# A new written-out order of steps, new evacuation engines and a new table of array parts for a fused H3 and FFN kernel on one core

## The chip, the core and the metric

The kernel runs on one core of a Trainium2 chip. A core has five engines that take instructions in order, each from its own queue: PE (TensorE, matmuls into PSUM), ACT (ScalarE, activation functions and copies), DVE (VectorE, elementwise work), POOL (GpSimd, some elementwise work and the issue of some DMAs) and SP (SyncE, here the issue of most DMAs). They wait for each other through semaphores. The metric is the device time of one execution in microseconds, lower is better.

## The reference

Inputs are `q`, `k`, `v` of 2048 x 640 in bfloat16, small filters, and the weights of a feed-forward net with 1728 hidden units. `_B_setup`'s own input is not used: both parts take the normalised `q`.

```python
xn = _layernorm(A_q)
# part A: H3
k_shift = sum over t of k_pad[t:t+S] * shift_k[ks-1-t]     # 4 taps
kv = k_shift * v
y = irfft(rfft(kv, 2S) * rfft(ssm_k, 2S))[:S] + kv * ssm_D  # long causal convolution
s = xn * y
# part B: FFN
g = silu(gelu(xn @ w1 + b1) @ w2 + b2)
return A_q + s * g
```

## The kernel before

**The opening.** `prologue` loads the first quarter of `q` and `w1`, normalises that quarter, transposes it and runs the first six column blocks of the first FFN matmul. On POOL it also computes, in `small_second`, the phases `ph` and the masks from which the 32 x 32 matrices of the short transform (`mats`) are made. The change leaves the opening as it is.

**The steps.** Everything behind the opening is one long string, `PLAN`, of 1190 steps. A loop at the end of the kernel calls one small function for each step, in the order written. Each engine's queue, and with it the order in which each engine works, is thus the order of the plan; so is which PSUM bank (of eight, `ones`) and which SBUF slot (`slots`) a step gets, since they are taken from and given back to lists as the steps are called. A step's name is a kind, a number and, where two engines can do it, the engine: `a` is ACT, `d` is DVE. `evac` (L145 to L148) does such a copy out of PSUM on the one or the other.

The kinds that matter here, with the lines of the profile of before:

- Layer norm of chunks 1 to 3 (a chunk is a quarter of the rows): `ls` statistics (DVE, L418 and L419), `lv`, `lr` (POOL), `lb`, `ln` the normalising itself (ACT L439 or DVE L441), `tt` transposes (PE L448), `te` their copy out (L147 or L148).
- FFN: `h` one column block of the first matmul (PE, L464; the last and narrow one of a chunk L460), `he` its gelu (ACT, L476 and L473), `g` one half row block of the second matmul (PE, L497, 14 matmuls), `ge` its silu (ACT, L505), `gm` the product with xn (DVE, L512). `h` and `g` steps 0 to 13 and 0 to 7 are those of chunk 0, and so on.
- Convolution filter: `kt` transposes of `ssm_k` (PE, L536), `kc` their copy out, `kf` the long first transform (PE, L547), `ke` its copy out, `ks` store to the DRAM scratch `scrK` (POOL), `fl` load back (SP), `ff` the short transform in 32-row blocks (PE, L411), `fe` its copy out, `mk` a copy with neighbouring rows swapped (SP).
- `kv`: `cv` the 64 steps of taps and products (DVE, L580, L587, L591), `em` and `ee` the taps spread over the partitions, then `uf`, `ue`, `us` (scratch `scrU`), `ml`, `mu` as for the filter.
- Spectrum and inverse: `mp` and `mq` the two products (DVE, L671), `ma` and `mb` the short inverse in 32-row blocks (PE, L411), `me` its copy out, `ms` store to `scrC` (POOL, L701), `yl` load back (SP, L708), `y` the long inverse (PE, L716 and L717), `yt` the product with xn * g (DVE, L725), `yo` and `ga` the last additions, `ys` and `gs` the stores.
- Tables of sines: `w` the phase of the first transform (`f1_phase`, DVE, L308), `ws` its sines (ACT), `s` the phase of `mats` (`small_phase`, DVE, L381 and L382), `ss` its sine (ACT, L387), `sm` the multiplication with the masks (DVE, L391). `ip`, `ia` (DVE, L618, L622) and `is`, `ib`, `ic` (ACT, L626, L630, L634) make the four tables of the last inverse, where `ia` needs `ip`.

**What binds the order.** All 16 `ks` stores must be in `scrK` before any `fl` load, and likewise for `scrU` and `scrC`, because the scratch is written by rows of one kind and read by rows of another. So no `y` can begin before the last `me` has been stored and read back. Gelu and silu lie in different tables of ACT; each change from one to the other is an `ACT_TABLE_LOAD`.

**The array parts.** A step of 32-row blocks is four matmuls of 32 x 32, one for each strip of rows, each on one of the 16 parts of the array. `TURNS` gives for each of the 48 column tiles which parts these are:

```python
for i in range(P // QB):
    j = (i + int(TURNS[turn])) % (P // QB)
    a, b = (slice(x * QB, (x + 1) * QB) for x in ((i, j) if m == F2 else (j, i)))
    nc.tensor.matmul(out=out[b, :], lhsT=mats[a, m, a], rhs=rhs[a, :], start=start, stop=stop)
```

Of the kernel before, what the change touches and what calls it, by code (L numbers as in the profile page):

```python
# [36 lines left out]
lv1 s cv8 cv17 cv9 he6 lr1 lb1 C4 he13 ee6.a cv18 cv19 cv10 ln4.d h10 he11 he10 h7 he7 h12 h9 ln5.a he12 ln7.a ln6.d  # L37
cv0 cv20 tt9 tt7 C1 C3 C0 he9 C2 cv11 cv1 te7.d cv21 ws0 tt6 tt8 te8.d g1 tt5 te9.d ss sm cv12 cv2 cv3 te5.d K3 X2 V5
K2 V4 V0 V3 V6 g0 ws1 ws2 ge0 ge1 g2 ge2 d kt1 kt7 kt6 kc7.a kt3 kt0 cv22 cv4 te6.d kc6.d kt2 kt9 kc3.d kc2.d kc0.a V2
X3 V7 kc9.d kc1.a kt12 kt4 kf2 kf23 kt11 kf8 ke2.d kc12.a V1 kt13 kc4.d kc13.d kf0 ke23.a ke8.a gm0.d kf6 kf22 ke6.a  # L40
ke22.a kt5 kf10 kf38 kc11.d ke0.d kt8 kf4 kc8.d kc5.d ke10.a ke38.a kf9 kt10 ke9.a ke4.a kt15 kc15.d kc10.d kt14 kf1
kf17 kc14.a kf11 kf40 ke17.a ke40.a kf15 kf29 kf18 kf21 ke11.a ke18.a ke15.a cv32 gm2.d cv13 gm1.d ke29.a g3 ke21.a
ke1.a kf45 kf7 kf5 kf35 kf20 ke45.a ke5.a kf19 ke19.a ke7.a ke35.a ke20.a ge3 kf16 g4 kf3 ge4 ke3.a ks7 ks0 ks2 kf39
kf37 cv24 ks6 ks1 ke39.a ke37.a kf27 cv33 cv23 cv34 cv5 cv35 ls10 gm3.d cv25 cv36 cv48 kf14 kf25 ke16.a ke27.a ke25.a
# [12 lines left out]
ff25 ue23.a fe12.a ff16 ff28 ff13 ff8 ff6 ff21 fe13.a fe6.a ff23 ff43 fe8.a fe28.a ff35 fe25.d fe2.d fe16.d us7 ff7
fe23.d fe21.d ff46 ff15 ff31 fe43.a fe7.a ln8.d gm10.d ls14 fe15.a fe46.a fe35.a fe31.a us12 gm9.d ln11.d g11 ge11 ff9
ff3 ff47 ff10 fe10.a fe47.d fe3.d ff4 ff33 ff20 fe33.a fe20.a tt13 ff24 fe24.a fe4.a mk2 fe9.d te13.d ff11 tt11 tt14
fe11.a te14.d tt10 te11.d te10.d ml2 ls13 ff34 ff29 ff1 ff37 fe34.a fe37.a ml1 ml3 mk1 ff44 ff14 ff42 fe14.d mk3 ml4  # L60
ml0 fe42.a fe29.a tt12 fe1.a te12.a fe44.a ls15 g12 gm11.d lv3 lr3 ge12 ml8 mu7 mp7 ff0 mu6 ff26 ff27 ff32 mu8 mp6
fe0.a fe32.a fe27.a fe26.a mp8 mq8 mq7 mq6 g14 mu11 ff45 ff17 ff18 mu9 fe45.a lb3 fe17.a fe18.a ln14.a g13 mp9 mp11
mq11 mq9 ge13 mu5 ge14 ma8 mb8 mu4 ma7 ff19 mb7 ff30 mu10 mp5 mp4 mq5 gm12.d mk8 mk4 mq4 g15 me8.a fe19.a fe30.a
ln15.a me7.a mk0 mu12 ff36 mu13 ma9 mu25 mp10 mb9 mu24 ge15 mq10 mp12 mq12 mp24 mq24 mp13 mq13 mp25 h39 h29 fe36.a
he39 me9.a he29 h28 ma11 mu26 mu14 ma5 mu2 mb5 mq25 mb11 ln13.a h30 ml5 ml6 ml7 mk6 fl13 he28 me5.a h32 he30 me11.a
ma24 mu3 ma10 mu18 mb24 mb10 mk5 mk7 ml9 mk12 q5 mk9 mp14 mp2 mp26 mq26 mq2 he32 me24.a ln12.a h40 mk14 ml11 he40
me10.a mp3 mp18 mq14 mq18 mq3 h34 ma2 mu19 mu23 mp23 ff41 mb2 he34 mq23 ff40 mu16 ff39 fe41.a fe40.a me2.a fe39.a h31
mu15 mu1 ma18 ma13 mb13 mb18 mp19 mq19 h41 mp1 mp16 mq1 he31 me18.a he41 me13.a mp15 h35 he35 ma4 mq16 mu17 ma12 ml12
mb4 mp17 mb12 me4.a me12.a h36 ma14 ma19 mu0 mq17 mb19 mq15 ma6 ma16 mu22 mb16 mb14 mb6 he36 mp0 mq0 me19.a me16.a
me6.a me14.a h37 mu27 ma15 ma26 mb26 mb15 mu28 mu21 h33 mp22 mq22 me26.a he37 he33 mp27 mp28 mq28 ml13 me15.a mq27  # L70
mk10 h38 he38 mp21 mq21 tt15 mu20 ma1 mb1 ml14 mu40 mp20 mp40 mu38 mk13 ml15 q2 q6 me1.a tt16 tt19 tt17 g17 te17.a
te16.a te19.a te15.a mp38 ma38 mq38 mb38 ma40 ma28 gm13.d mq40 mq20 mu43 mu37 me38.a ma3 mb28 mb40 mb3 mu41 g16 me40.a
me28.a me3.a mp37 mq37 mp43 mk11 ma27 ml10 mu35 mp41 mq41 ge16 gm14.d ma0 ma17 mb27 mb0 mb17 mu34 me0.a me17.a gm15.d
mp35 mp34 mq34 ge17 me27.a mk15 q0 g18 mq43 ge18 mq35 gm17.d ma25 ma23 mu36 ma34 mb25 mb23 mb34 mp36 mu29 mu31 tt18
me34.a me25.a me23.a te18.a mp29 gm16.d mq29 mq36 mp31 mq31 g19 ma21 mu32 q3 ma29 ma41 mu47 mb21 mb29 mb41 g20 me29.a
mp47 mq47 me41.a ge19 ma20 mu39 ma37 ma36 me21.a mu30 mb37 mb20 mb36 mp32 mq32 ir ge20 g21 ma32 mp39 me37.a me20.a
me36.a ma39 mu33 ma43 mp30 mq39 gm18.d mq30 ge21 mb32 ma31 ma47 mb39 ms0 ms5 ms3 ms9 ms2 ms8 ms1 ms12 mb43 mb31 mb47
mu45 g22 me39.a me31.a me47.a ms4 me43.a me32.a ms6 ms13 ma35 gm19.d mp33 mq33 mp45 mq45 ma33 ma22 ip1 ia1 ma30 mb35
mb33 mb22 ge22 mb30 mu42 mu44 mu46 me22.a me35.a me33.a me30.a ms7 is1 ib1 h43 h53 h50 mp42 mp46 mp44 mq42 mq44 mq46
ma44 ms10 ma42 ma45 gm21.d ma46 mb44 mb42 mb45 mb46 ms11 me46.a me44.a ic1 me45.d me42.d g23 gm20.d h48 h42 he42 h46  # L80
he50 h49 h55 he49 he48 h44 he46 h52 he43 he52 h51 he44 he51 he55 h54 ms14 gm22.d h45 ms15 yl5 he53 he54 he45 h47 yl7
yl6 y11 y9 y10 ip2 he47 g24 yl12 yl4 q1 yl1 yl2 ip3 ip0 ia2 yt11 ia0 ia3 yl0 is0 ib0 is3 ib3 ic0 y7 yt10 yt7 yt9 yo3.d
ge23 g25 ge24 ge25 y6 y2 yt2 gm23.d y8 y0 y1 yt0 yt1 yl11 ic3 y18 yt6 yt8 yt18 yo2.d yo0.d is2 ib2 ic2 y3 g27 y17 yl9
y14 yl13 yl3 y5 yt14 yt5 y19 y4 yt4 yl14 y21 yt21 yt19 yt17 yt3 yl8 g29 y12 yt12 y20 y13 yo1.d gm24.d yl15 y23 yt13
yt23 yt20 ys0 ys3 q4 yl10 y15 y16 g26 y22 g28 yt15 ge26 yt16 yo5.d gm25.d ga25 yt22 ys1 q7 yo4.d ge27 ge28 gm28.d
gm26.d ga24 ga26 ys2 g30 gs25 g31 ys5 ge29 gm27.d ge30 ge31 gm29.d ga27 ga28 gs27 gm30.d ga30 ga29 gs30 gs29 gm31.d
ga31 gs31 ys4
"""


# [1 line left out]
def kernel(  # L92
# [314 lines left out]
    def blocks(out, m, rhs, turn, start=True, stop=True):  # L407
# [500 lines left out]
```

## Time and profile before

| | us |
|---|---|
| median of 3 runs (lowest, highest) | 197.5 (197.5, 198.28) |
| profiled execution | 197.71 |
| its span | 195.9 |
| PE busy | 187.5 |
| DVE busy | 174.0 |
| ACT busy | 162.6 |
| POOL busy | 49.0 |

The granted TensorE clock was 1.0 of full speed in the profiled execution. A row of a group gives line, engine and operation, the tiles written and read, the count, then busy time, the mean of one in ns, and the idle time of that engine just ahead of them with what ended it. Operations of one engine overlap a little, so busy time over count is less than the mean of one. A row of the timeline starts with its start and its length in us. All on-chip buffers that hold rows are named `area`, and all of PSUM is `banks`.

### The profile page before, as it was taken

The page shows a single profiled execution, that of the slowest core. Times are in us where ns is not written, and L with a number is a line of the kernel's source. Part 1 is how long each engine was busy: PE and PEld are TensorE (multiplying, and loading weights), DVE is VectorE, ACT ScalarE, POOL GpSimd, SP SyncE. Part 2 cuts the span into 40 slices and gives each one's busy share as a digit, 9 for nine tenths or more (in the row PEclk, how much of TensorE's full clock was granted, in tenths as well). Part 3 has the DMA queues.
Part 4 walks back from the last instruction along what each step waited for, and adds up shares of the span by engine and source line. Part 5 has one row for each costly group of instructions (what it writes and reads, how often), then busy time and mean ns, then how long its engine had stood idle before and what let it go on. Part 6 is the DMA issues. An engine that isn't in the chain of part 4 may idle for free.

```text
span 195.9 us, 5143 instructions
## 1 busy us (share of the span) xinstructions
PE 187.5 (96%) x1939; PEld 111.3 (57%) x1939; DVE 174.0 (89%) x371; ACT 162.6 (83%) x323; POOL 49.0 (25%) x85
## 2 busy tenths in 40 slices
PE   7999989899999999998999999999999999999992
PEld 2485457776665455663565443365665544657772
DVE  6989997999999999989999999999999920389993
ACT  3478999999999999999998999999779758991041
POOL 8545100004554032354031000000466410002220
PEclk9999999999999999999999999999999999999999
DMA  6999999964888899798788999597869759995344
GB/s 204 402 371 350 361 408 412 395 254 152 319 326 342 237 363 364 298 347 345 261 273 296 302 341 323 165 280 256 259 241 335 250 156 329 371 402 215 136 167 174
DMA packets 26401, 57.69 MB, mean 294 GB/s; under 512 B 3016, under 2 KB 14857, under 8 KB 26376
## 3 DMA queue, kind: packets, MB, share of 16 engines
q1 hardware_dynamic: 21872, 39.65, 58.0%
q0 software_dynamic: 4320, 17.70, 24.4%
q8 instruction: 15, 0.25, 0.6%
q14 instruction: 10, 0.08, 0.1%
q10 hardware_dynamic: 184, 0.01, 0.1%
HBM read 33.76 MB, written 18.35 MB: 266 GB/s over the span
## 4 chain that ended last, share of the span: by engine, by line
PE 71%; ACT 18%; DVE 7%; issue 3%; POOL 0%; POOLq 0%; ACTq 0%; DVEq 0%
PE banks L497 23%; PE banks L464 21%; ACT area L147 8%; PE banks L411 7%; PE banks L547 5%; ACT hT L476 4%; PE banks L783 3%; PE banks L536 2%; PE banks L716 2%; PE banks L448 2%; ACT sl L505 2%; PE banks L717 2%; DVE area L587 2%; DVE area L304 1%; PE banks L460 1%
## 5 line engine op out<-in xcount | busy, mean ns | idle before, releaser
L147 ACT CAST area<-banks 128x426 bf16<-128x426 f32 (+2 forms) x175 | 80.7, 629 | 3.9 <-PE banks L411 3.4
L497 PE MATMUL banks<-w_sb,hT 128*128 128x320 bf16 (+1 forms) x462 | 65.7, 295 | 0.5 <-ACT sl L505 0.4
L497 PEld LDWEIGHTS <-hT 128*128 128x128 bf16 x462 | 43.5, 98 | 19.1 <-issue 4.1
L464 PE MATMUL banks<-xnT,w_sb 128*128 128x512 bf16 x230 | 53.6, 379 | 0.1
L671 DVE TENSOR_TENSOR area<-banks,area 128x426 bf16<-128x426 f32 (+1 forms) x96 | 50.2, 594 | 0.2
L476 ACT ACTIVATE hT<-banks,b_f 128x512 bf16<-128x512 f32 x52 | 35.4, 719 | 4.8 <-PE banks L464 3.0
L464 PEld LDWEIGHTS <-w_sb 128*128 128x128 bf16 x230 | 21.6, 98 | 25.7 <-issue 3.7
L505 ACT ACTIVATE sl<-banks 128x320 bf16<-128x320 f32 (+1 forms) x33 | 15.0, 480 | 14.2 <-PE banks L497 12.9
L591 DVE TENSOR_TENSOR area<-area 128x1280 bf16<-128x1280 bf16 x32 | 25.4, 818 | 0.3
L701 POOL DMA_DIRECT2D scrC<-area x16 | 11.7, 732 | 42.1 <-ACT area L147 39.9
L411 PE MATMUL banks<-area,mats 32*32 32x426 bf16 (+1 forms) x768 | 20.7, 345 | 0.5 <-DVE area L148 0.2
L725 DVE TENSOR_TENSOR area<-banks,xn 128x426 bf16<-128x426 f32 (+1 forms) x18 | 10.0, 595 | 12.4 <-ACT hT L476 10.2
L587 DVE TENSOR_TENSOR area<-area 128x1280 bf16<-128x1280 bf16 x24 | 19.1, 814 | 0.0
L562 POOL DMA_DIRECT2D scrK<-area x16 | 8.9, 557 | 31.8 <-DVE area L591 25.1
L547 PE MATMUL banks<-area,WA 128*128 128x212 bf16 (+1 forms) x64 | 15.6, 299 | 0.0
L547 PE MATMUL banks<-area,WB 128*128 128x214 bf16 (+1 forms) x64 | 15.3, 299 | 0.0
L411 PEld LDWEIGHTS <-mats 32*32 32x32 bf16 x768 | 8.1, 88 | 12.4 <-issue 9.7
L148 DVE CAST area<-banks 128x426 bf16<-128x426 f32 (+1 forms) x21 | 11.4, 594 | 1.8 <-PE banks L411 0.8
L573 POOL DMA_DIRECT2D scrU<-area x16 | 8.7, 546 | 14.7 <-ACT area L147 13.8
L734 POOL DMA_DIRECT2D out_dram<-area x6 | 3.3, 549 | 29.4 <-DVE area L730 21.9
L418 DVE BATCH_NORM_STATS2 st<-xn 128x6 f32<-128x320 bf16 x24 | 10.4, 473 | 0.0
L512 DVE TENSOR_TENSOR xn<-xn,sl 128x320 bf16<-128x320 bf16 (+1 forms) x33 | 9.8, 308 | 0.2 <-ACT sl L505 0.2
(108 smaller groups left out, 202.0 us busy)
## 6 DMA issues: line engine op xcount, KB each, us to landing
scrK<-area POOLq DMA_DIRECT2D x16, 320.0 KB, 3.3
scrU<-area POOLq DMA_DIRECT2D x16, 320.0 KB, 3.6
area<-scrK SPq DMA_DIRECT2D x16, 320.0 KB, 6.4
area<-area SPq DMA_DIRECT2D x32, 160.0 KB, 4.1
area<-scrU SPq DMA_DIRECT2D x16, 320.0 KB, 3.9
scrC<-area POOLq DMA_DIRECT2D x16, 320.0 KB, 4.3
area<-scrC SPq DMA_DIRECT2D x16, 320.0 KB, 6.5
area<-in_A_k_dram SPq DMA_DIRECT2D x4, 640.0 KB, 10.0
```

The costliest lines, as they stand in the source:

```text
L147: return nc.scalar.copy(out=out_ap, in_=in_ap)
L148: return nc.vector.tensor_copy(out=out_ap, in_=in_ap)
L411: nc.tensor.matmul(out=out[b, :], lhsT=mats[a, m, a], rhs=rhs[a, :], start=start, stop=stop)
L464: nc.tensor.matmul(out=ps, lhsT=w1_sb[:, t, ft * P:(ft + 1) * P], rhs=xnT[:, t, :], start=(t == 0), stop=(t == DT - 1))
L476: nc.scalar.activation(out=hT[:, ft, :], in_=one(("h", i)), func=ACT.Gelu_apprx_tanh, bias=b1_f[:, ft:ft + 1], scale=1.0)
L497: nc.tensor.matmul(out=ps[:, 0:ws.stop - ws.start], lhsT=hT[0:M, ft, q * P:(q + 1) * P], rhs=w2_sb[0:M, ft, hs.start + ws.start:hs.start + ...
L505: nc.scalar.activation(out=sl[:, ws], in_=one(key)[:, 0:ws.stop - ws.start], func=ACT.Silu)
L547: nc.tensor.matmul(out=ps[:, dst], lhsT=(WA, WB)[r][:, n2, :], rhs=rows[:, n2 % 2, src], start=True, stop=True)
L587: nc.vector.tensor_tensor(out=uc, in0=uc, in1=tmp, op=ALU.add)
L591: nc.vector.tensor_tensor(out=tmp if s else uc, in0=kh[:, r0:r0 + KC, :], in1=w_exp[:, j:j + 1, :].to_broadcast([P, KC, D]), op=ALU.mult)
L671: nc.vector.tensor_tensor(out=flat(("p", i))[:, x * w:x * w + w], in0=one(("mu", i))[:, 0:w], in1=flat(key)[:, cols(j)], op=ALU.mult)
L701: nc.gpsimd.dma_start(out=pair_view(scrC)[g2], in_=pair(("c", g2)))
```

## The change

The table `TURNS` is another one, and the plan has the same 1190 steps in another order, with the engine letter of some copies changed. The opening, the step functions and all arithmetic stay. Since the plan is one line shorter, every line number behind it is one less in the profile of the changed kernel (L380 there is L381 here).

```diff
-TURNS = "231221331312001123202202330111320201303303312100"
+TURNS = "331023121031002102313332203331230123011120302102"
...
-em6 he0 he1 w X1 em7 em5 he2 K1 em4 ls6 ls7 ls4 ls5 K0 h11 he5 ee5.a ee4.a h8 h6 he4 ee7.a he3 he8 B1 h13 B2 B0 cv16
...
+h11 s X1 he0 he2 w h13 em5 em6 he4 he3 em4 he1 he5 em7 ee7.a ee5.a he11 h9 K1 K0 ls7 ls4 ls6 ls5 ee6.d lv1 cv16 h6 B0
...
-ma44 ms10 ma42 ma45 gm21.d ma46 mb44 mb42 mb45 mb46 ms11 me46.a me44.a ic1 me45.d me42.d g23 gm20.d h48 h42 he42 h46
...
+mu42 mb47 mb32 mb35 me32.a q5 h43 h49 mq46 mp42 me35.a me47.d mq42 ma42 ma46 ma45 ms12 ms8 ma44 ms13 mb42 mb46 mb45
+ip1 ms7 me45.a me46.a ms11 ms10 ms6 ms15 mb44 me44.a me42.a ms14 h44 h51 g23 h47 h46 ia1 gm20.d is1 ib1 ic1 he53 he46
...
```

The number of copies on each engine, over the whole plan:

| kind | ACT before | DVE before | ACT now | DVE now |
|---|---|---|---|---|
| `ee` | 4 | 0 | 3 | 1 |
| `ln` | 6 | 6 | 5 | 7 |
| `te` | 6 | 9 | 9 | 6 |
| `kc` | 5 | 11 | 6 | 10 |
| `ke` | 46 | 2 | 43 | 5 |
| `ue` | 41 | 7 | 40 | 8 |
| `fe` | 38 | 10 | 37 | 11 |
| `me` | 46 | 2 | 46 | 2 |

Up to the last product (`mq46` before, `mq42` now) DVE does none of its two `me` before and both now (`me33.d`, `me47.d`); `ip1` and `ia1` stand ahead of that product before and behind it now. Runs of 32-row steps, with other PE work on both sides, are 26 before and 29 now.

The first place is DVE just behind the opening, whose last instruction is the copy into `dD_sb`. Before, from that copy to the phase of `mats`:

```order
L852 COPY dD_sb<-banks 128x5
L308 TENSOR_SCALAR area<-area 128x2048
L418 BN_STATS st_297<-xn 128x6 x2
...
L591 TENSOR_TENSOR area<-area 128x1280
L423 TENSOR_SCALAR ve_352<-mv_298 128x4
L381 TENSOR_SCALAR area<-area 128x384
L382 TENSOR_SCALAR area<-area 128x384
```

And now, from the same copy:

```order
L851 COPY dD_sb<-banks 128x5
L380 TENSOR_SCALAR area<-area 128x384
L381 TENSOR_SCALAR area<-area 128x384
L307 TENSOR_SCALAR area<-area 128x2048
L417 BN_STATS st_328<-xn 128x6 x2
L418 BN_AGGR mv_329<-st_328 128x2
```

The two instructions of `s` moved from behind the statistics of chunk 1 to the first place, ahead of `w` and of everything else that DVE does behind the opening.

The second place is DVE around its last products; `area<-banks,area` is a product, `area<-banks` a copy out, `kn,kj` the index table of `ip`. Before:

```order
L671 TENSOR_TENSOR area<-banks,area 128x428 x4
L618 SCALAR_TENSOR_TENSOR area<-kn,kj 128x512
L622 TENSOR_SCALAR area<-area 128x512
L671 TENSOR_TENSOR area<-banks,area 128x428
L671 TENSOR_TENSOR area<-banks,area 128x426 x2
L671 TENSOR_TENSOR area<-banks,area 128x428
L671 TENSOR_TENSOR area<-banks,area 128x426 x2
L512 TENSOR_TENSOR xn<-xn,sl_2409 128x320
L148 CAST area<-banks 128x428 x2
```

And now:

```order
L670 TENSOR_TENSOR area<-banks,area 128x426 x2
L147 CAST area<-banks 128x428
L670 TENSOR_TENSOR area<-banks,area 128x426 x3
L670 TENSOR_TENSOR area<-banks,area 128x428
L147 CAST area<-banks 128x426
L670 TENSOR_TENSOR area<-banks,area 128x428
L617 SCALAR_TENSOR_TENSOR area<-kn,kj 128x512
L621 TENSOR_SCALAR area<-area 128x512
```

Two copies of `me` moved ahead of the last products, and the index table moved behind them.

The third place is ACT at the same point of the plan, with the last copies of `me`, the sine table and the change to the gelus of chunk 3. Before:

```order
L147 CAST area<-banks 128x428 x2
L626 ACTIVATE WB<-area,sin_bias 128x512
L630 ACTIVATE area<-area,half_l 128x512
L147 CAST area<-banks 128x426 x2
L634 ACTIVATE WA<-area,sin_bias_h 128x512
L476 ACT_TABLE_LOAD
L476 ACTIVATE hT<-banks,b_f 128x512 x9
```

And now:

```order
L146 CAST area<-banks 128x426 x4
L146 CAST area<-banks 128x428
L146 CAST area<-banks 128x426 x2
L146 CAST area<-banks 128x428
L625 ACTIVATE WB<-area,sin_bias 128x512
L629 ACTIVATE area<-area,half_l 128x512
L633 ACTIVATE WA<-area,sin_bias_h 128x512
L475 ACT_TABLE_LOAD
```

The whole sine table moved behind the last copy of `me`, of which the last four are now all on ACT.

More of the change, by code (lines that the diff above doesn't have):

```diff
@@ L40 @@
[L40 to L44, printed above, removed]
@@ L75 @@
[L75 to L79, printed above, removed]
@@ L85 @@
[L85 to L87 removed]
+h11 s X1 he0 he2 w h13 em5 em6 he4 he3 em4 he1 he5 em7 ee7.a ee5.a he11 h9 K1 K0 ls7 ls4 ls6 ls5 ee6.d lv1 cv16 h6 B0
+B1 B2 ee4.a he9 he13 he6 cv8 lr1 cv17 lb1 cv9 h12 h8 h7 he12 ln5.a he8 cv0 cv1 ln7.d cv10 ln4.d ln6.d h10 cv18 cv19 C3
+tt7 tt5 tt8 tt6 he7 he10 g0 tt9 g1 te6.d te5.d te8.d cv20 C1 C0 C4 C2 ws0 ss ge0 cv2 cv11 cv3 sm cv21 te9.d ws1 ge1
```

83 lines of the change are left out of this document (46 added, 37 removed).

## The prediction

> **What bounds the kernel now.** I read the page first: the busy shares, then the chain that ended last.
>
> ```profile
> span 195.9 us, 5143 instructions
> PE 187.5 (96%) x1939; PEld 111.3 (57%) x1939; DVE 174.0 (89%) x371; ACT 162.6 (83%) x323; POOL 49.0 (25%) x85
> PE 71%; ACT 18%; DVE 7%; issue 3%; POOL 0%; POOLq 0%; ACTq 0%; DVEq 0%
> ```
>
> No single engine carries the span: the chain lies on PE for 71% and changes to ACT and DVE for 25%. The profiled execution took 197.71 us, 1.81 around its span, and lies 0.2 above the median of 197.5; I sum against 197.71 and take off 0.2 at the end. Next I asked for busy time by stage, cut where the kernel's phases change: the end of the opening, the small sine, just behind the last f1 tiles of kv, the last product of the spectrum, the first matmul of the final inverse.
>
> ```profile
> core 0: us, PE busy (x) PEld busy (x) DVE busy (x) ACT busy (x) POOL busy (x), PEclk, DMA share, GB/s
> 13.10:31.00 17.90, 16.93 (x125) 10.41 (x124) 16.54 (x37) 15.98 (x26) 5.08 (x6) 1.00 1.04 369
> 31.00:92.50 61.50, 60.14 (x489) 37.68 (x486) 60.13 (x111) 61.37 (x131) 19.09 (x33) 1.00 0.86 316
> 92.50:153.70 61.20, 60.65 (x986) 32.42 (x970) 60.51 (x132) 55.89 (x117) 12.55 (x20) 1.00 0.84 279
> 153.70:168.30 14.60, 14.60 (x111) 7.21 (x111) 3.91 (x10) 11.24 (x19) 1.56 (x3) 1.00 0.74 252
> ```
>
> The reader should see three things. From 31.0 to 153.7 DVE is busy 120.64 of 122.70 us. ACT has no room in the first of these stages (61.37 of 61.50) and some in the second (55.89 of 61.20). PE is nearly as full, but the page warns that a busy PE is not one at its peak, so its share hides waits. Behind 153.7 DVE has 10 us free, while PE is full. DVE takes its instructions in the order written and must pass every one ahead of its last product before PE can make the last inverse blocks. So I count on DVE: its start, plus its work, plus its waits, up to that product, and behind it the tail on PE. These are all its waits in that stretch:
>
> ```profile
> DVE mats L391 <- ACT area L387: 1.1, 1, 1.1
> DVE area L148 <- PE banks L411: 0.8, 2, 0.5
> DVE area L148 <- ACT area L147: 0.5, 1, 0.5
> DVE area L148 <- PE banks L547: 0.4, 2, 0.2
> ```
>
> 2.8 us together: no order of the same work can gain more than that on this engine.
>
> **The change, term one: DVE's first step behind the opening.** Before, DVE goes from the opening straight to `f1_phase` (L308), and `small_phase` (L381) comes 6 us later. The change puts `small_phase` first. It reads `ph`, whose last writer is POOL's L373.
>
> ```profile
> 13.08 0.15 DVE L852 COPY dD_sb<-banks 128x5 bf16<-128x5 bf16 x1
> 13.14 1.22 DVE L308 TENSOR_SCALAR area<-area 128x2048 int32<-128x2048 int32 x1
> 19.05 0.36 DVE L381 TENSOR_SCALAR area<-area 128x384 int32<-128x384 f32 x1
> 12.21 0.61 POOL L369 TENSOR_SCALAR area<-area 128x128 f32<-128x128 f32 x1 [4.27 <-DVE area L360]
> 12.92 1.59 POOL L372 TENSOR_SCALAR area<-area 128x128 f32<-128x128 f32 x1
> 14.58 0.61 POOL L373 TENSOR_SCALAR area<-area 128x128 f32<-128x128 f32 x1
> ```
>
> L373 ends at 15.19 and DVE would be there at 13.14, so the new wait is at most 2.05 us. Queued behind it is everything DVE does: the statistics of chunk 1, then its norms, then PE's transposes. But L372 took 1.59 us where L369 and L373, on the same 128x128 f32, took 0.61, and it is just the one that lay beside DVE's L308. With L308 no longer running at that time, L372 may take 0.61 and the wait be 2.05 - 0.98 = 1.07 us. I take 1.1, since both neighbours of L372 ran at 0.61, and keep 2.05 as the other end. The Trainium skill, SBUF — State Buffer, section "Who interferes with whom", says that GpSimd and a DVE operation in a two-port mode share one port pair as an exclusive lock and the second fully blocks, with tensor_scalar among those that can take it; L372's 1.59 us agrees with that, and by a reading without the lock the forecast below would be 199.8 instead of 198.8.
>
> **Term two: the wait for `mats` goes.** In the rows above DVE waits 1.1 us at L391 for ACT's small sine. In the new order three kv steps (`cv2`, `cv11`, `cv3`) stand between ACT's sine and DVE's use of it, and DVE arrives later by term one. Minus 1.1; at the worst nothing is gained.
>
> **Term three: more work on DVE ahead of its last product.** The letters of the plan give, up to the last product: plus 7 casts (fe +1, ue +1, ke +3, me +2), plus one norm, plus one tap copy, minus one kT copy, minus three xnT copies; and `ip1` and `ia1` move behind it, where DVE is idle.
>
> ```profile
> L148 DVE CAST area<-banks 128x426 bf16<-128x426 f32 (+1 forms) x21 | 11.4, 594 | 1.8 <-PE banks L411 0.8 <-ACT area L147 0.5 <-PE banks L547 0.4
> L148 DVE COPY area<-banks 128x640 bf16<-128x640 bf16 x11 | 4.8, 483 | 0.0
> L148 DVE COPY xnT<-banks 128x512 bf16<-128x512 bf16 x9 | 3.4, 418 | 0.0
> L441 DVE TENSOR_SCALAR xn<-xn,mv,rs 128x640 bf16<-128x640 bf16 x6 | 2.6, 441 | 0.0
> L618 DVE SCALAR_TENSOR_TENSOR area<-kn,kj 128x512 int32<-128x512 int16 x4 | 2.6, 684 | 0.0
> L622 DVE TENSOR_SCALAR area<-area 128x512 int32<-128x512 int32 x4 | 1.6, 421 | 0.0
> ```
>
> I price by busy time over count, because successive operations overlap. 7 x 11.4/21 = 3.80; norm 2.6/6 = 0.43; the tap copy (320 wide, no DVE row) between 0.38 and 0.54, I take 0.4; kT 4.8/11 = 0.44; three xnT 3 x 3.4/9 = 1.13; `ip1` 2.6/4 = 0.65, `ia1` 1.6/4 = 0.40. Sum 3.80 + 0.43 + 0.4 - 0.44 - 1.13 - 0.65 - 0.40 = +2.0 us. Nothing covers it, as DVE was busy 98% of that time.
>
> ACT is given relief by the same letters:
>
> ```profile
> L147 ACT CAST area<-banks 128x426 bf16<-128x426 f32 (+2 forms) x175 | 80.7, 629 | 3.9 <-PE banks L411 3.4
> L439 ACT ACTIVATE xn<-xn,nb,rs 128x640 bf16<-128x640 bf16 x6 | 5.6, 936 | 0.0
> L147 ACT COPY xnT<-banks 128x512 bf16<-128x512 bf16 x8 | 4.6, 613 | 2.3 <-PE banks L774 1.8 <-PE banks L448 0.2 <-PE banks L848 0.2
> L147 ACT COPY area<-banks 128x640 bf16<-128x640 bf16 x5 | 3.3, 751 | 0.0
> ```
>
> Over the whole kernel six casts fewer, 6 x 0.46 = 2.8, one norm fewer 0.93, one kT copy more 0.66, three xnT copies more 1.7: minus 1.3 us. I do not add it: it shortens ACT, and pays only where DVE waits.
>
> **Term four: DVE's other waits.** 1.7 us of L148 waits remain above. A lighter ACT feeds DVE earlier, and 0.5 of them name ACT; I take minus 0.5, from minus 1.7 (all gone) to plus 1.7 (the five waits average 0.34, and the plan has five more casts on DVE that could wait as long).
>
> **Term five: the tail.** Between the last inverse block and the first matmul of the final inverse both orders give PE one `ffn2`, ten full `ffn1` and the narrow one, 13.5 us, which cover the round trip through `scrC`.
>
> ```profile
> 154.18 2.08 PE L497 MATMUL banks<-w_sb,hT 128*128 128x320 bf16 x14
> 167.66 0.34 PE L716 MATMUL banks<-area,WA 128*128 128x426 bf16 x1
> 155.97 1.45 POOL L701 DMA_DIRECT2D scrC<-area  x2 [2.17 <-ACT WA L634]
> 159.91 2.23 SPq L708 DMA_DIRECT2D area<-scrC  x5
> area<-scrC SPq DMA_DIRECT2D x16, 320.0 KB, 6.5
> 154.38 0.93 ACT L147 CAST area<-banks 128x426 bf16<-128x426 f32 x2 [0.95 <-PE banks L411]
> L634 ACT ACTIVATE WA<-area,sin_bias_h 128x512 bf16<-128x512 f32 x4 | 2.9, 722 | 0.0
> 168.68 1.28 ACT L315 ACT_TABLE_LOAD   x1
> PEld L716 <- ACT WA L634: 0.8, 2, 0.6
> ```
>
> The loads start at 159.91 and take 6.5: 166.4, 1.2 us ahead of 167.66. Now the last four casts all stand on ACT, 0.93 us later, but one store instead of two follows them, so the loads keep their time. ACT then runs the three instructions of the last sine table in a row (each like L634's 0.72; two of them stood earlier) ahead of the gelus, whose first is so some 2.4 us later than it could be before (0.93 + 2 x 0.72), less what ACT waited there for PE. ACT's last gelu must wait for PE's last `ffn1` (167.66) in both orders, so its end near 168.68, where the next table load starts, stays, and PE meets the final sines two `ffn2` (3.8 us) later than before: the 0.8 us for L634 can go, of which PE itself lost some. I take minus 0.2, from minus 0.4 to plus 1.5 if ACT comes too late.
>
> **PE's own cost.** There are 29 runs of 32-row blocks instead of 26.
>
> ```profile
> 86.40 0.39 PE L411 MATMUL banks<-area,mats 32*32 32x426 bf16 x12
> 86.72 0.35 PE L547 MATMUL banks<-area,WA 128*128 128x428 bf16 x1
> 153.66 0.58 PE L411 MATMUL banks<-area,mats 32*32 32x426 bf16 x32
> ```
>
> Three groups held PE 0.32 us (86.40 to 86.72), eight held it 0.52 (153.66 to 154.18): 0.04 a group and 0.2 a run. Three runs more are 0.6 us. I cost them at nothing, as PE waits on DVE there; without that cover it is 0.6.
>
> **Sum:** 1.1 - 1.1 + 2.0 - 0.5 - 0.2 = +1.3: 199.0 for an execution like the profiled one, 198.8 for the median.
>
> **Rivals.**
> *ACT sets the pace up to 92.5, and its relief pays: faster.* For it speaks 61.37 of 61.50. It needs DVE to swallow its extra work in the waits it had, which it can only if the new wait at the start is near nothing and the L148 waits vanish. Then minus 1.3 from ACT and minus 0.2 in the tail: 196.0. It decides where DVE's start slips by less than 0.5 us.
> *The work fits into the waits: no change.* 1.1 - 1.1 + 2.0 - 1.7 - 0.4 = -0.1: 197.4. Against it: every wait would have to go at once.
> *DVE's start is fully late.* POOL's L372 keeps its 1.59, and the sum of 2.05 - 1.1 + 2.0 - 0.5 + 0 is +2.5: 200.0; with term four at its other end as well, 2.05 - 1.1 + 2.0 + 1.7 = +4.7, 202.2.
> *PE is the bound after all.* Then DVE's terms are hidden behind it and only its runs count: +0.6, 198.1. Against it speak the 25% of the chain that are not on PE. The Trainium skill, TensorEngine Tiling (Array Packing), section "Key Properties", has the mechanism: a change of tiling mode drains the array. The 0.2 us a run agrees with it.
>
> **How the numbers follow.** Forecast 0.45; fully late 0.17; no change 0.16; PE 0.08; faster 0.14. A measurement of this kernel tells about 0.5% (1.0 us) from no change, so 196.5 and 198.5 are the bounds. Faster 0.14, within 0.24, slower 0.62. The range leaves out about one in ten on either side: 196.6 to 201.4; the forecast's own is 198.2 to 199.6.
>
> **What would show it.** The first step: DVE waits for POOL's L372 (373 before) at about 13.1, for 1.1 us. The second: no wait at the `mats` row. The third: 26 casts in DVE's group, and busy time up to the last product 2.0 us more, that product ending near 155. The tail: the first inverse matmul 13.5 us behind the last block. It is wrong if DVE shows idle time in the middle stages and yet the end comes earlier, which would mean that ACT or PE, not DVE, set the pace.

## The result and the profile after

The changed kernel takes 196.81 us (median of 7 runs, 196.72 to 196.91) against 197.5 us before: a ratio of 0.9953, 95% interval 0.9938 to 0.9968. It is faster by 0.7 us by the medians, 0.9 by the ratio. I had forecast 1.3 us slower. The profiled execution has a span of 195.1 us, 0.8 less than before.

The page of the changed kernel, busy shares and the chain that ended last:

```profile
span 195.1 us, 5140 instructions
PE 186.0 (95%) x1927; PEld 110.8 (57%) x1939; DVE 174.9 (90%) x374; ACT 161.8 (83%) x320; POOL 49.3 (25%) x85
PE 78%; DVE 16%; issue 2%; POOL 1%; ACT 1%; POOLq 0%; DVEq 0%; ACTq 0%
```

ACT's share of the chain fell from 18% to 1%, and DVE's rose from 7% to 16%. (In `h_after_head`, described below, whose order is the same up to the last product, they are 5% and 17%.) Busy time by stage, in the same columns as before (PE, weight load, DVE, ACT, POOL):

```profile
31.00:92.50 61.50, 60.22 (x497) 37.98 (x499) 61.22 (x111) 60.64 (x129) 17.93 (x33) 1.00 0.88 324
92.50:153.40 60.90, 60.43 (x963) 31.95 (x980) 60.38 (x133) 53.92 (x113) 12.36 (x20) 1.00 0.86 285
```

In the stage from 31.0 to 92.5, where the filter and kv are transformed, DVE and ACT have changed places. Before, ACT was busy 61.37 of 61.50 us and DVE 60.13; now DVE has 61.22 and ACT 60.64. DVE's waits of 0.4 us and more behind the opening and up to the last product are these two (line, what it waits for, sum, count, longest):

```profile
DVE area L380 <- POOL area L372: 0.6, 1, 0.6
DVE area L670 <- PE banks L410: 0.4, 1, 0.4
```

The wait for `mats` is gone, and so are all five waits of DVE's copies that stood among the rows of before. How this adds up is read from one row of each kernel: the stretch from where DVE's first step behind the opening could start (13.14 before; 13.42 now, as in both this is 0.06 to 0.07 us behind the start of the opening's last copy) to the end of its last product. First before, then after, then a third kernel, `h_after_head`, that has the changed order up to there. It serves as a second execution of that order.

```profile
13.14:153.65 140.51, 137.63 (x1569) 80.44 (x1567) 137.09 (x277) 133.24 (x272) 36.63 (x59) 1.00 0.88 307
```

```profile
13.42:153.32 139.90, 136.98 (x1575) 79.89 (x1583) 138.18 (x280) 130.08 (x265) 35.66 (x58) 1.00 0.89 311
```

```profile
13.55:153.43 139.88, 137.73 (x1585) 79.93 (x1583) 138.33 (x280) 130.07 (x265) 35.59 (x57) 1.00 0.89 311
```

DVE has 3 instructions and 1.09 us more work. What it is not busy falls from 140.51 - 137.09 = 3.42 us to 139.90 - 138.18 = 1.72. That stretch starts 0.28 later. So the last product ends 0.28 + 1.09 - 1.70 = 0.33 us earlier (153.32 against 153.65). The tail behind it takes 195.1 - 153.32 = 41.78 against 42.25: 0.47 less. Together that is the 0.8 us. ACT has 3.16 us less work in that stretch, of which 1.5 are the two instructions of the sine table (0.75 and 0.72) that now stand behind the last product.

### The profile page after: what moved, and what is told of

It reads as the page before. It is cut to its first block, busy times and chain, and to the rows that moved or that the text cites. A ratio compares the mean times of both kernels' runs of the same rounds, so it can differ in the third digit from the quotient of the medians.

```text
span 195.1 us, 5140 instructions
## 1 busy us (share of the span) xinstructions
PE 186.0 (95%) x1927; PEld 110.8 (57%) x1939; DVE 174.9 (90%) x374; ACT 161.8 (83%) x320; POOL 49.3 (25%) x85
## 4 chain that ended last, share of the span: by engine, by line
PE 78%; DVE 16%; issue 2%; POOL 1%; ACT 1%; POOLq 0%; DVEq 0%; ACTq 0%
PE banks L496 28%; PE banks L463 22%; PE banks L546 9%; PE banks L410 9%; DVE area L590 3%; PE banks L535 2%; PE banks L715 2%; PE banks L716 2%; DVE area L586 2%; DVE st L417 2%; PE banks L447 2%; DVE stats L744 1%; DVE area L303 1%; DVE area L147 1%; DVE xnT L147 1%
## 5 line engine op out<-in xcount | busy, mean ns | idle before, releaser
L146 ACT CAST area<-banks 128x426 bf16<-128x426 f32 (+2 forms) x169 | 76.7, 570 | 5.4 <-PE banks L410 4.3
L475 ACT ACTIVATE hT<-banks,b_f 128x512 bf16<-128x512 f32 x52 | 34.2, 708 | 2.5 <-PE banks L782 1.4
L590 DVE TENSOR_TENSOR area<-area 128x1280 bf16<-128x1280 bf16 x32 | 24.8, 813 | 0.2
L586 DVE TENSOR_TENSOR area<-area 128x1280 bf16<-128x1280 bf16 x24 | 18.9, 812 | 0.0
L546 PE MATMUL banks<-area,WA 128*128 128x428 bf16 (+1 forms) x64 | 16.1, 298 | 0.2
L147 DVE CAST area<-banks 128x426 bf16<-128x426 f32 (+2 forms) x27 | 14.9, 583 | 0.0
```

What stands on the lines that cost most here:

```text
L146: return nc.scalar.copy(out=out_ap, in_=in_ap)
L147: return nc.vector.tensor_copy(out=out_ap, in_=in_ap)
L475: nc.scalar.activation(out=hT[:, ft, :], in_=one(("h", i)), func=ACT.Gelu_apprx_tanh, bias=b1_f[:, ft:ft + 1], scale=1.0)
L546: nc.tensor.matmul(out=ps[:, dst], lhsT=(WA, WB)[r][:, n2, :], rhs=rows[:, n2 % 2, src], start=True, stop=True)
L586: nc.vector.tensor_tensor(out=uc, in0=uc, in1=tmp, op=ALU.add)
L590: nc.vector.tensor_tensor(out=tmp if s else uc, in0=kh[:, r0:r0 + KC, :], in1=w_exp[:, j:j + 1, :].to_broadcast([P, KC, D]), op=ALU.mult)
```

## The experiments

The expectations speak of three theories. D: DVE alone sets the pace up to its last product, as the prediction had it. P: PE sets it together with DVE, so that its 32-row runs count. A: before, ACT set the pace of the early stages, and its relief is what paid. Later ones add F: each engine letter fits the steps around it, so that a single one can't be priced. Gains and losses against the changed kernel are worked out as (ratio - 0.9953) x the median of before on the same chip; by the intervals of the two ratios they are known to some 0.4 us.

### The three parts of the change, one at a time

**The table.** `e2_old_turns` is the changed kernel with the table of before.

```diff
-TURNS = "331023121031002102313332203331230123011120302102"
+TURNS = "231221331312001123202202330111320201303303312100"
```

> The new plan with the old table of array parts, all else unchanged. Going through the runs of 32-row steps in the order written, with 0.014 us from one group to the next, 0.165 us where a group uses array parts that an earlier one of the run still holds, and 0.28 us behind the last, the runs add up to 15.7 us with the new table and 19.2 us with the old one. Theory D (DVE sets the pace up to its last product, PE waits on it): at most +0.5 us against the new kernel, since PE has room. Theory P (PE, through its 32-row runs, sets the pace as much as DVE): +2 to +3.5 us.

Measured: 199.62 us, ratio 1.0087 (1.0070 to 1.0103), 2.65 us slower than the changed kernel. The groups of the 32-row matmuls by shape (busy time, mean of one in ns, idle time ahead), before, after and with the old table in the new order:

```profile
L411 PE MATMUL banks<-area,mats 32*32 32x426 bf16 x512 | 19.2, 345 | 0.5 <-DVE area L148 0.2
L411 PE MATMUL banks<-area,mats 32*32 32x428 bf16 x256 | 13.3, 346 | 0.1
```

```profile
L410 PE MATMUL banks<-area,mats 32*32 32x426 bf16 x512 | 19.1, 345 | 0.5
L410 PE MATMUL banks<-area,mats 32*32 32x428 bf16 x256 | 13.3, 346 | 0.0
```

```profile
L410 PE MATMUL banks<-area,mats 32*32 32x426 bf16 x512 | 20.8, 344 | 0.5
L410 PE MATMUL banks<-area,mats 32*32 32x428 bf16 x256 | 15.3, 344 | 0.1
```

The same 768 matmuls hold PE 32.4 us with the table made for the order and 36.1 us with the other, each one as long as before (344 to 346 ns): the time lies in how they overlap. The starts in the traces, read beside the plan and the table, say more. Of the 192 groups of four, 10 before and 12 in the changed kernel use array parts that the group just ahead in the run uses, and 35 do here. Such a group starts a median of 0.13 to 0.18 us behind the one ahead in these three kernels; one that shares no part with either of the two groups ahead starts 0.014 us behind. DVE then waits for PE at its products, where the changed kernel has one such wait of 0.4 us:

```profile
DVE area L670 <- PE banks L410: 1.4, 3, 1.0
```

3.7 us of PE work became 2.65 us of time. Theory P holds, and D in its pure form does not: PE has about 1 us of room against DVE.

**The table in the old order.** `b_new_turns` is the kernel before with the new table alone (the diff above, the other way round, in the order of before).

> The kernel before with the new table of array parts, nothing else. Summed by 0.014 us between two groups of a run, 0.165 where a group starts on an array part that the group ahead of it uses, and 0.28 behind a run, the 32-row runs cost PE 19.1 us instead of 15.2. Theory P (PE co-sets the pace): slower by 2 to 4 us, as the old table was in the kernel after (2.8 us slower there for 3.5 us by the rule). Theory D as the prediction had it (the runs lie hidden behind DVE): within 0.5 us of the kernel before. It also says whether either table is better by itself: if the new one were, this would be faster than before.

Measured: 200.39 us, ratio 1.0134 (1.0104 to 1.0164), 2.6 us slower than before (0.0134 x 197.6).

```profile
L411 PE MATMUL banks<-area,mats 32*32 32x426 bf16 x512 | 21.3, 344 | 0.6 <-DVE area L148 0.2
L411 PE MATMUL banks<-area,mats 32*32 32x428 bf16 x256 | 14.6, 344 | 0.2 <-ACT area L147 0.2
```

35.9 us against 32.5. Here 36 of the groups use parts of the group just ahead, and start a median of 0.09 us behind it. Neither table is better by itself; each fits its own order. The new table gains nothing over before: it keeps in the new order what the old table had in the old one. PE's group is 32.4 us now and was 32.5, with three runs more; since the table changed with the runs, what three runs cost by themselves is not shown.

**The letters.** `e4_old_letters` is the changed kernel, order and table, with every copy on the engine where it was before.

```diff
-h11 s X1 he0 he2 w h13 em5 em6 he4 he3 em4 he1 he5 em7 ee7.a ee5.a he11 h9 K1 K0 ls7 ls4 ls6 ls5 ee6.d lv1 cv16 h6 B0
+h11 s X1 he0 he2 w h13 em5 em6 he4 he3 em4 he1 he5 em7 ee7.a ee5.a he11 h9 K1 K0 ls7 ls4 ls6 ls5 ee6.a lv1 cv16 h6 B0
...
```

> The new plan's order and table, but each copy on the engine that it had before (only letters change): by the prediction's prices about 1.9 us less work on DVE and 1.3 us more on ACT than in the new kernel. Theory D: faster than the new kernel by 0.5 to 1.9 us. Theory A (the relief of ACT is what pays): slower by 0.7 to 1.3 us.

Measured: 205.3 us, ratio 1.0373 (1.0353 to 1.0392), 8.3 us slower. That is a miss for both theories: D expected it faster, since DVE gets less work, and the 1.3 us of work that A counts for ACT explain a sixth of it. The two largest of DVE's waits:

```profile
DVE xn L511 <- ACT sl L504: 4.6, 2, 3.0
DVE area L147 <- PE banks L410: 2.8, 1, 2.8
```

DVE now stands for 3.0 us in front of a `gm` whose silu lies behind a row of copies on ACT. The sum of work on each engine says little about an order in which a copy stands on the other engine than the one it was placed for.

### The first step, and the tail

**`s` later.** `e1_s_late` is the changed kernel with `s` moved behind `cv16`, some 5.5 us later, where DVE need not wait for POOL.

```diff
-h11 s X1 he0 he2 w h13 ... ee6.d lv1 cv16 h6 B0
+h11 X1 he0 he2 w h13 ... ee6.d lv1 cv16 s h6 B0
```

> The new plan with the one step s moved back behind the statistics of chunk 1 (behind cv16), where it stood before. DVE's wait of 0.64 us for POOL ahead of everything goes. Theory D: 0.4 to 0.7 us faster than the new kernel, unless the wait at mats comes back (it was 1.1 us in the kernel before). Theory A: no change, within 0.2 us.

Measured: 196.38 us, ratio 0.9922 (0.9900 to 0.9945); by the ratios 0.6 us faster than the changed kernel, with an uncertainty of 0.5. The opening in the changed kernel, DVE and POOL (start, length):

```profile
13.35 0.15 DVE L851 COPY dD_sb<-banks 128x5 bf16<-128x5 bf16 x1
14.14 0.36 DVE L380 TENSOR_SCALAR area<-area 128x384 int32<-128x384 f32 x1 [0.64 <-POOL area L372]
14.82 1.31 DVE L307 TENSOR_SCALAR area<-area 128x2048 int32<-128x2048 int32 x1
...
12.89 0.53 POOL L371 TENSOR_SCALAR area<-area 128x128 f32<-128x128 f32 x1
13.50 0.61 POOL L372 TENSOR_SCALAR area<-area 128x128 f32<-128x128 f32 x1
14.10 0.95 POOL L373 TENSOR_SCALAR area<-area 128x128 f32<-128x128 f32 x1
```

And POOL in `e1_s_late`, where DVE's L307 runs from 13.18 to 14.51:

```profile
13.50 1.47 POOL L372 TENSOR_SCALAR area<-area 128x128 f32<-128x128 f32 x1
```

POOL's L371 and L372 (L372 and L373 before) take 0.53 to 0.61 us alone, and 1.47 here and 1.59 before where L307 ran beside one of them. With L307 gone from its side, L371 took 0.53 instead of 1.59, and DVE could start `s` at 14.14. The chain of this argument held. What it cost is seen in the last product of `e1_s_late`, and in the waits that did not come back:

```profile
13.14:152.47 139.33, 137.56 (x1585) 79.91 (x1584) 138.28 (x280) 129.90 (x265) 35.48 (x58) 1.00 0.88 312
```

DVE has the same 280 instructions and is idle only 1.05 us. Its last product ends at 152.47, 0.85 earlier than in the changed kernel. Its opening ended 0.24 sooner, which would not have helped the changed kernel: in the runs with `s` first whose last copy of the opening started at 13.05 to 13.07, `s` still started at 14.14 to 14.16, behind POOL. So `s` in the first place costs time, but takes up the scatter of the opening. The seven runs of the changed kernel lie within 0.19 us and those of `h_after_head` within 0.15, the four of `e1_s_late` within 0.88. `e1_s_late` and `e5_me_on_act`, which is below, were the fastest orders.

**The tail.** `h_after_head` is the changed kernel up to `mb44`, with the remaining steps in the order and with the letters of before.

```diff
 ip1 ms7 me45.a me46.a ms11 ms10 ms6 ms15 mb44
-me44.a me42.a ms14 h44 h51 g23 h47 h46 ia1 gm20.d is1 ib1 ic1 he53 he46
+ia1 is1 ib1 h50 gm21.d me44.a ic1 me42.d g23 gm20.d h48 h42 he42 h46
...
```

> The new plan up to its last inverse block (mb44), and behind it all remaining steps in the order that they had before. Theory D: the tail is worth what the traces show between DVE's last product and the end, 41.78 against 42.25 us, so 0.3 to 0.5 us slower than the new kernel. If the tail is not where part of the gain lies: the same within 0.2 us.

Measured: 197.09 us, ratio 0.9959 (0.9943 to 0.9974), 0.1 us more than the changed kernel. In its profile PE's load waits for the last sine table as it did before, which the changed kernel does not do:

```profile
PEld L715 <- ACT WA L633: 0.8, 2, 0.6
```

Yet its whole tail takes 195.3 - 153.43 = 41.87 us, against 42.25 before and 41.78 after. That figure holds the last stores, and from the start of DVE's last addition to the end of the span it is 2.7 to 3.0 us in the profiles of all these kernels, 3.00 before and 2.74 in `h_after_head`. These are the last additions before, after and in `h_after_head`:

```profile
192.90 0.24 DVE L520 TENSOR_TENSOR xn<-xn,area 128x160 bf16<-128x160 bf16 x1
```

```profile
192.14 0.24 DVE L519 TENSOR_TENSOR xn<-xn,area 128x160 bf16<-128x160 bf16 x1
```

```profile
192.56 0.24 DVE L519 TENSOR_TENSOR xn<-xn,area 128x160 bf16<-128x160 bf16 x1
```

From the end of the last product to there it is 39.25, 38.82 and 39.13 us. So the tail's own new order is worth 0.3 us in the profile, as theory D had it, and what comes along with the order ahead of it 0.1. The ratios, at 0.1 with an uncertainty of 0.4, cannot tell.

### Which engine sets the pace, measured with idle work

Four kernels add work that nothing reads to the changed kernel, either five statistics on DVE or ten small copies on ACT, once between `g4` and `g6` (kv stage) and once between `g18` and `g20` (spectrum stage); two do the first to the kernel before.

```diff
+    def pad_dve():
+        nc.vector.bn_stats(out=padd[:], in_=w1_sb[:, 0, 0:320])
+    def pad_act():
+        nc.scalar.copy(out=pada[:], in_=w1_sb[:, 0, 0:32])
...
-ke41.a kf47 kf37 gm3.d kf36 ke47.a ke36.a kf3 g4 gm2.d ke3.a
+ke41.a kf47 kf37 gm3.d kf36 ke47.a ke36.a kf3 g4 pd gm2.d ke3.a
```

> The kernel after, with five idle statistics of 128x320 on DVE spread between g4 and g6 (early kv stage, some 30 to 60 us); nothing reads them. By the rows of L417 and L418 one is some 0.42 us, together 2.1 us. Theory D (DVE sets the pace there): DVE's last product and the end move by 1.7 to 2.1 us, so 198.5 to 198.9 against 196.8. Theory A (ACT sets the pace there, DVE has been fed late before and has room): up to 0.7. Theory P (PE co-sets the pace, its queue is as full as DVE's): between, 0.7 to 1.5, with PE waiting more for DVE.

> The kernel after, with ten idle copies of 128x32 on ACT spread over the same place (g4 to g6), some 0.2 us each, together 2 us; nothing reads them. Theory D: ACT is off the path, 0 to 0.4 us. Theory A (ACT sets the pace there, so that its relief is what paid): 1.5 to 2 us. Theory P: 0.3 to 1.2, since PE's banks are emptied later.

> The kernel after, with the same five idle statistics on DVE spread between g18 and g20 (spectrum stage, some 120 to 145 us), 2.1 us. Theory D: 1.7 to 2.1 us. Theory P: 0.7 to 1.5. Theory A: up to 0.7.

> The kernel after, with the same ten idle copies on ACT spread between g18 and g20, 2 us. ACT was busy 53.9 of 60.9 us there and idle 1.9 us ahead of the last me casts. Theory D: 0 to 0.4 us. Theory P: 0.2 to 0.8. Theory A: 1.5 to 2 us.

> The kernel before, with five idle statistics of 128x320 on DVE between g4 and g6, as in the same run of the kernel after (there five of 0.48 us cost 2.1 us). Theory D, the prediction's (before, DVE sets the pace, its waits are 2.8 us in all): +2.0 to +2.4 us. Theory A (before, ACT set the pace there: 61.37 us busy of 61.50, and DVE has room): +0.3 to +1.2. If the two were level in both kernels: +1.5 to +2.

> The kernel before, with ten idle copies of 128x32 on ACT between g4 and g6; in the kernel after ten of 0.30 us, 3.0 us together, cost 1.5 us. Theory D: 0 to 0.6 us. Theory A (ACT had less room before than after, so that its relief is part of what was gained): 2.0 to 3.0, clearly more than in the kernel after. If ACT had the same room in both: 1.3 to 1.7.

The added work has to be taken as busy time, since successive operations overlap. It is read from the row that starts with DVE's first step and ends with its last product, in the changed kernel with the addition on DVE and on ACT in the kv stage:

```profile
14.16:155.64 141.48, 137.55 (x1576) 78.84 (x1574) 140.18 (x283) 130.04 (x265) 35.27 (x56) 1.00 0.86 305
```

```profile
14.16:154.75 140.59, 136.56 (x1576) 79.12 (x1574) 138.34 (x278) 130.94 (x275) 35.04 (x56) 1.00 0.87 307
```

and in the kernel before:

```profile
13.43:154.83 141.40, 137.24 (x1559) 80.42 (x1567) 138.90 (x282) 133.34 (x272) 36.16 (x58) 1.00 0.87 305
```

```profile
13.14:154.80 141.66, 137.73 (x1559) 80.47 (x1567) 137.16 (x277) 134.36 (x282) 36.51 (x59) 1.00 0.87 304
```

and in the spectrum stage of the changed kernel, DVE and ACT:

```profile
14.37:155.04 140.67, 137.23 (x1576) 78.89 (x1574) 139.96 (x283) 129.57 (x265) 35.03 (x56) 1.00 0.87 307
```

```profile
14.14:153.58 139.44, 136.52 (x1576) 79.05 (x1574) 138.25 (x278) 130.72 (x275) 34.97 (x56) 1.00 0.88 310
```

The changed order's own row, from its first step at 14.14, is that of `h_after_head`, whose instructions up to there are the same:

```profile
14.14:153.43 139.29, 137.14 (x1580) 79.40 (x1578) 138.24 (x278) 129.90 (x265) 35.00 (x56) 1.00 0.89 311
```

| run | ratio (95%) | busy time added | time added | share |
|---|---|---|---|---|
| before, kv stage, DVE | 1.0048 (1.0028 to 1.0069) | 138.90 - 137.09 = 1.81 | 0.95 | half |
| before, kv stage, ACT | 1.0054 (1.0040 to 1.0069) | 134.36 - 133.24 = 1.12 | 1.07 | all |
| after, kv stage, DVE | 1.0056 (1.0041 to 1.0071) | 140.18 - 138.24 = 1.94 | 2.04 | all |
| after, kv stage, ACT | 1.0025 (1.0015 to 1.0034) | 130.94 - 129.90 = 1.04 | 1.42 | all |
| after, spectrum, DVE | 1.0030 (1.0017 to 1.0044) | 139.96 - 138.24 = 1.72 | 1.52 | most |
| after, spectrum, ACT | 0.9965 (0.9950 to 0.9980) | 130.72 - 129.90 = 0.82 | 0.24 | little |

The times are uncertain by 0.3 to 0.4 us, so that the last one is not clear of nothing. The ends of DVE's last product, with a later start of its first step taken off, agree: they come 0.9 and 1.15 us later in the kernel before, and 2.2, 1.3, 1.4 and 0.15 later in the changed one.

Before, ACT set the pace of the kv stage: its added work counted in full, and DVE's by half, as its waits took in the rest (141.40 - 138.90 = 2.50 us not busy, where it had 3.42). That is theory A for the kernel before; my expectation of 2 to 3 us for it was off because I had counted each copy at 0.30 us and not at the 0.11 by which ACT's busy time grew. In the changed kernel DVE and ACT are level there, so that work on either counts. In the spectrum stage ACT has room and DVE has little, as theory D says, though 1.52 us is less than the 1.7 to 2.1 that I expected by it.

### Single letters, from the fastest order

If added work costs its length, does work taken away give it back? `e5_me_on_act` and `e6_ke_on_act` start from `e1_s_late` and move two `me` casts ahead of the last products, or three `ke` casts of the kv stage, from DVE to ACT.

```diff
-ge22 mb43 h53 me43.a me22.a ms9 mp44 me33.d ... mp42 me35.a me47.d mq42
+ge22 mb43 h53 me43.a me22.a ms9 mp44 me33.a ... mp42 me35.a me47.a mq42
```

```diff
-ke17.d ke28.a ke29.a kf30 kc15.d kc1.d ke12.d ke27.a ... ke31.d
+ke17.a ke28.a ke29.a kf30 kc15.d kc1.d ke12.a ke27.a ... ke31.a
```

> The kernel after with s behind cv16 (196.4 us on the chip of that run, 0.6 faster than after), and its two me casts on DVE (me33, me47, 0.59 us each, just ahead of the last products) given to ACT, which waits for PE at that place anyway. Theory D, with the prices measured with idle work in this stage (0.65 to 0.85 of the work for DVE, 0.1 for ACT): 1.2 us of DVE work less is worth 0.7 to 1.0 us, 0.1 us back on ACT: 0.6 to 0.9 us faster than that kernel. Theory F (the letters fit the order; ACT takes the copy later, and its bank and the store of me wait): no gain or up to 1 us slower.

> The same kernel, with three of the five ke casts on DVE (ke17, ke12, ke31; before there were two in all) given to ACT, in the kv stage. Term three of the prediction priced them at 0.54 us each on DVE: 1.6 us faster by theory D alone. With the prices of idle work in this stage (1.0 of its length on DVE, 0.5 on ACT): 3 x 0.54 less 3 x 0.47 x 0.5 = 0.9 us faster. Theory A (ACT full: 28.82 us busy of 29.00 there) and theory F (fitted letters): 0 to 1.4 us slower.

`e5_me_on_act`: 196.36 us, ratio 0.9925 (0.9904 to 0.9947), the same as `e1_s_late` (0.9922). Its last products on DVE (six in a row) and PE's last run of inverse blocks:

```profile
148.65 3.15 DVE L670 TENSOR_TENSOR area<-banks,area 128x426 bf16<-128x426 f32 x6 [0.40 <-PE banks L410]
...
150.49 2.33 PE L463 MATMUL banks<-xnT,w_sb 128*128 128x512 bf16 x10
152.75 0.58 PE L410 MATMUL banks<-area,mats 32*32 32x428 bf16 x32
```

The same in `e1_s_late`:

```profile
151.86 0.59 DVE L670 TENSOR_TENSOR area<-banks,area 128x428 bf16<-128x428 f32 x1
...
150.12 2.33 PE L463 MATMUL banks<-xnT,w_sb 128*128 128x512 bf16 x10
152.38 0.58 PE L410 MATMUL banks<-area,mats 32*32 32x428 bf16 x32
```

DVE's last copy of the opening started at 13.50 and 13.11 in these two executions. Counted from there, DVE ends its last product 138.30 and 139.34 us later, 1.04 sooner without the two casts; PE starts its last run 139.25 and 139.27 us later. PE is busy with ten matmuls of the first layer just ahead of that run, so the earlier product finds it busy. At this place PE and DVE are level: more work on DVE costs, less of it pays nothing.

`e6_ke_on_act`: 197.0 us, ratio 0.9961 (0.9947 to 0.9975), 0.8 us slower than `e1_s_late`. The place is a single wait:

```profile
DVE xn L511 <- ACT sl L504: 1.9, 1, 1.9
```

ACT's silu `ge3`, behind the three casts, comes 1.6 us later than in `e1_s_late`, of which 0.6 is an opening that ended later. DVE, with three casts less, is early for the product behind it and stands there 1.9 us. From that step on DVE is 1.5 us later, the same 0.6 included. Single letters do not add up either: the theory that they fit the steps around them holds in the kv stage, where ACT is full.

## Why the prediction was wrong

The argument that failed is the first one: that DVE alone sets the pace up to its last product, so that its terms add up at their full price. With it went the sizes of terms three and four. In the terms of the sum the profile has +1.0 for the start, -1.1 for `mats`, +1.1 for DVE's work, -1.3 for its other waits (3.42 - 1.1 = 2.3 before, 1.72 - 0.72 = 1.0 now, without the waits of terms one and two) and -0.5 for the tail: -0.8, where I had +1.3. Of the 2.1 us between, term three has 0.9, term four 0.8 and term five 0.3. Point by point:

- **Which engine counts.** I had read DVE's 120.64 of 122.70 us as the bound of both middle stages and put ACT's 61.37 of 61.50 aside as something that "pays only where DVE waits". The idle work shows that before the change ACT was the one whose work counted in full in the kv stage, and DVE's counted by half. The chain of waits had pointed that way, with 18% on ACT and 7% on DVE; I named these shares and then did not use them.
- **Term one, +1.1, right.** DVE's phase of `mats` started at 14.14, where its first step had started at 13.14. The wait in the profile is 0.64 because the opening ended 0.27 later in that execution; in the runs with this order whose opening ended as early as before it is 0.93. The lock that the Trainium skill, SBUF — State Buffer, section "Who interferes with whom", describes agrees with POOL's 0.53 us away from L307 and the 1.47 to 1.59 beside it. That the second of the two blocks, as the prediction has it, is not borne out: by the profile, in which POOL's spans are rough, L372 of the kernel before started 0.22 us ahead of L308 and was the one that took longer. The step costs: with `s` moved back the kernel is 0.6 us faster.
- **Term two, -1.1, right.** No wait stands at `mats` any more.
- **Term three, +2.0, too large, and its price wrong.** DVE's copies out of PSUM, up to the last product, are these before and in `h_after_head`:

```profile
13.14:153.65 140.51, 18.03 (x39) 1.00 0.88 307
```

```profile
13.48:153.43 139.95, 21.20 (x43) 1.00 0.89 311
```

That is 3.2 us more, where I had 3.80 + 0.4 - 0.44 - 1.13 = 2.6. Yet all busy time grew only by 1.09 us, or 1.24 in `h_after_head`. The rest is in operations that the change only moved:

```profile
L591 DVE TENSOR_TENSOR area<-area 128x1280 bf16<-128x1280 bf16 x32 | 25.4, 818 | 0.3
```

```profile
L590 DVE TENSOR_TENSOR area<-area 128x1280 bf16<-128x1280 bf16 x32 | 24.9, 820 | 0.2
```

The first row is before, the second `h_after_head`: 32 tap products, each as long, take 0.5 us less together. In the kernel before one sees how that can be:

```profile
57.15 0.82 DVE L587 TENSOR_TENSOR area<-area 128x1280 bf16<-128x1280 bf16 x1
57.89 0.82 DVE L580 TENSOR_TENSOR area<-area 128x1280 bf16<-128x1280 bf16 x1
...
62.94 0.82 DVE L587 TENSOR_TENSOR area<-area 128x1280 bf16<-128x1280 bf16 x1
63.79 0.83 DVE L591 TENSOR_TENSOR area<-area 128x1280 bf16<-128x1280 bf16 x1
```

L580 starts 0.74 us behind the start of the operation ahead of it, L591 0.85, though both follow an L587 of 0.82. In the second pair the two are successive steps of one chain of taps, and the product writes the buffer that the addition ahead of it has just read; in the first they belong to different chains. By the plan this holds for all neighbours among the 64 steps of `cv`: such pairs, 7 before and 4 now, do not overlap, and all others, 34 and 40, do. In the whole stretch 31 of DVE's operations do not overlap the one ahead of them before and 21 now: besides three such pairs, `ip1` and `ia1` are behind it now and three waits are gone. At some 0.08 us each, ten fewer are 0.8 us. The copies with my prices for the norm, `ip1` and `ia1` make 3.2 + 0.43 - 1.05 = 2.6 us, 1.5 more than measured; what the other 0.7 are stays open. That the shared buffer is what prevents the overlap fits every such pair, but no run tried it by itself. The sign of being wrong that I had named, idle time on DVE with an earlier end, did not show: DVE's idle time fell, and its work took less than I had priced. The price, "nothing covers it", was wrong as well: before, half of such work went into DVE's waits.
- **Term four, -0.5, mis-sized.** All the L148 waits went, 1.7 us, my lower end. One of 0.4 for PE came in. The reason I gave, that a lighter ACT feeds DVE earlier, agrees with ACT's smaller work up to there, and with what three casts given back to ACT cost; that it is the reason for each of these waits was not tried.
- **Term five, -0.2.** The tail is 0.47 shorter in the profile, 0.43 of it up to DVE's last addition, of which its own order has 0.3. The 0.8 us wait for the last sines went as forecast.
- **PE's own cost at nothing.** With three more runs PE's group is no longer than it was, but not because DVE hides PE: the table of array parts keeps the sum at 32.4 us, and 3.7 us more there cost 2.65. The rule that I weighed for the rival on PE (the Trainium skill, TensorEngine Tiling (Array Packing), section "Key Properties") says that a change of tiling mode drains the array, which would be paid by the run. No run here shows that price by itself; the same runs differ by 3.7 us through the table alone, which that rule does not tell.

Of the rivals, the one in which the work fits into the waits came nearest by the number, 197.4 us, and its terms four and five (-1.7 and -0.4) were near; what it had too much is term three. ACT's relief was the one with the right direction. It gave 196.0 us on the condition that DVE's start slips by less than 0.5. The start slipped by 1.0, and the kernel came to 196.81; without the slip, `e1_s_late`, its ratio 0.9922 makes 196.0 of the 197.5. I had put that rival at 0.14 because it needed the waits to vanish, which they did. That the two figures meet is partly luck: the rival priced ACT's relief at 1.3 us over the whole kernel, and taking it back in `e4_old_letters` cost 8.3.

## What to carry to other kernels

Where two or three engines are busy over 97% of a stage, none of them is the bound by that number: adding a little idle work to each, one at a time, tells which one counts, and taking work away from one of them pays only until the next is level. The shares of the chain of waits pointed the same way in the kernel before and should have weighed more than busy shares, but they are no measure: the changed kernel has 1% of its chain on ACT, and yet ACT's added work counts in full in its kv stage. Orders, engine letters and such tables as that of the array parts that were made together are to be costed as a whole; one of them undone alone told only how well it fits, not what it is worth.

## What the runs showed of the hardware

- Which of the 16 array parts the 32 x 32 matmuls use, and in which turn, moved the same 768 matmuls by 3.7 us (32.4 to 36.1), at 345 ns for each one. In the four kernels read for it above, groups that use parts of the group just ahead in the run start a median of 0.09 to 0.18 us behind it, and groups that share no part with the two ahead 0.014 to 0.026.
- The opening is the same in all these kernels, but its last copy on DVE started between 13.05 and 13.71 us in the profiled executions. A difference of less than 0.6 us between two single profiles is not to be read without that; the comparisons above count from that copy where it matters. An order whose first step waits for something later than that copy, as `s` does for POOL, hides this scatter.
- The identical order on DVE (after and `h_after_head`) ran with means of 813 and 820 ns for the same operation (L590) in two executions, 0.9% apart, while its busy time up to the last product differs by 0.1% (138.18 and 138.33 us): the length of single operations is not their price.
